# Attention scores formed one item ahead, and as one product of 128 keys instead of two of 64

## The chip, the cores and the metric

The kernel runs on one core of a Trainium2 chip. The metric is the device time of one execution in microseconds (us), as the median of several runs.

## What is computed

The first half is a linear attention with a decaying state, over batch 4, 8 heads, 768 tokens and a head dimension of 48, all in float32. The second half sends each of the 3072 tokens (384 features) to one of 8 experts.

```python
for t in range(S):                       # attention, for every batch b and head h
    cur = einsum('bhd,bhe->bhde', u * k[t], v[t])
    y[t] = einsum('bhd,bhde->bhe', r[t], state + cur)
    state = w[..., None] * state + einsum('bhd,bhe->bhde', k[t], v[t])
x = y transposed to (B, S, H * D)
logits = x @ w_gate                      # router: the best expert, or the one of the token before
out = p[e] * (relu(x @ w1[e]) @ w2[e])   # e is the token's expert, p its softmax share
```

## The kernel before

Two heads share the 128 partitions (64 each, 48 used), so an *item* is a batch and a pair of heads, and there are 16 items. An item's 768 tokens are six chunks of 128. `run` goes over the items in a loop whose order is written out by hand; each engine executes its instructions in that order, and the engines wait for each other by semaphores. After the loop come the experts, which are TensorE work almost without a break.

The steps of one item n, with the line numbers of the profile:

- `load` (L199, L203, L204, SP's queue): rk holds r and k with tokens along the free axis, kv holds k and v with tokens on the partitions, vT is v turned. It runs three items ahead.
- `scale` (GpSimd): rw = r times the decay to its place in the chunk (L234), pd = r times k (L221), ke = k times the decay to the chunk's end (L217). Items 0 to 2 get rw from VectorE. It is issued one item ahead.
- `keys` (VectorE, L241): kw = k divided by the decay.
- `added` (TensorE, L253) and `states` (VectorE, L259): what each chunk adds to the state, and the scan that makes the five states S.
- `scores` (TensorE, L288): products of kw and rw for each chunk and head, three chunks at a time (g = 0 and 1) into one of two pairs of PSUM banks; then `am` on VectorE (L290) multiplies them by the tile `kept`, which has zeros where a key doesn't come before the query.
- `own` (TensorE, L269): the token's own term, u times pd, into the PSUM tile y; VectorE multiplies it by vT in place (L273).
- `inside` (TensorE, L297): adds v times am to y. `before` (TensorE, L310): adds the states' part. Then ScalarE copies y to xT (L314). The tile y has one buffer, so own(n+1) waits for the copy of item n.
- `turn` (TensorE, L323; ScalarE, L325): xT back to tokens on the partitions, two items later, through a bank pair. After four items ScalarE's queue writes x to memory (L328), and `logits` (L336) and `token_logits` (L342) form the router's logits, also through the bank pairs.

`banks` hands out the two bank pairs in turn, so every user waits until the reader of what stood there has finished.

In iteration n the order on TensorE is: turn(n-2), added(n), inside(n-1), before(n-1), scores(n), own(n). The masked scores of item n are thus made in iteration n and used in iteration n+1. Each chunk's score product is split into two of 64 keys. The first half of the keys meets all 128 queries, the second half only the last 64, since no key comes after its query. The two halves are written to different halves of the PSUM partitions, swapped in odd chunks; so `kept` has an entry for even and one for odd chunks, and v, k and the decay table for ke come with swapped halves there (`_tokens`, `endT`).

Between these steps stand the steps of the router for the first two batches: `keys` and `runs` in iteration 10 (L679, L684), `turn_runs` at the end of 10 (L689), `last` and `one_hot` in 11, `counts` and `ranks` in 12, `slots` and `places` in 13 and 14 (L765 to L783), `summed` and `head` in 15 (L790, L800); after `head` the first tokens are gathered for the experts (L1037).

Of the kernel before, what the change touches and what calls it, by code (L numbers as in the profile page):

```python
# [11 lines left out]
F32 = mybir.dt.float32  # L12
# [8 lines left out]
P = 128  # L21
B, H, S, DH = 4, 8, 768, 48
HP = H // 2
DP = 64
U = DP + DH
D = H * DH
E, F = 8, 1024
DK, FK = D // P, F // P
NCH = S // P
NC = B * NCH  # L30
# [20 lines left out]
C2 = NCH // 2  # L51
# [4 lines left out]
def spread(ap, axis, n):  # L56

    a = ap.unsqueeze(axis)
    return a.to_broadcast([n if i == axis else s for i, s in enumerate(a.shape)])


class Attention:
# [10 lines left out]

    def __init__(self, tc, st, rk_d, kv_d, vT_d, x_d, w_t, wp_d, kept, ident, lt, mp):
        self.tc, self.nc = tc, tc.nc
        nc = tc.nc
        self.rk_d, self.kv_d, self.vT_d, self.x_d = rk_d, kv_d, vT_d, x_d
        self.w_t, self.kept, self.ident, self.lt = w_t, kept, ident, lt  # L80

        self.late = st.enter_context(tc.tile_pool(name="late", bufs=1))
        self.wp = self.late.tile([P, H, 32], F32, name="wp")
# [3 lines left out]
        def pool(name, bufs, **kw):  # L87
            return self.inner.enter_context(tc.tile_pool(name=name, bufs=bufs, **kw))

        once = pool("once", 1)  # L90
        self.two = pool("two", 2)
        self.three = pool("three", 3)
        ps = pool("ps", 1, space=PSUM)

        self.pairs = [ps.tile([P, 2, 512], F32, name=f"pair{i}") for i in range(2)]
# [7 lines left out]
        n = B * HP - 1  # L103
# [25 lines left out]
        n = 2  # L129
# [7 lines left out]
        nc.scalar.copy(self.first, tab[:, 0, 0])  # L137
        self.reciprocals(0)

        self.end = once.tile([P, HP, P + DP], F32, name="end")  # L140
        self.endT = once.tile([P, 2, HP, 2 * DH], F32, name="endT")
        self.align(26)
        self.warm(8)
        self.ends(slice(0, 1))
# [19 lines left out]
            self.nc.tensor.transpose(t[:, i % 2, :P], self.ident, self.ident)  # L164

    def ends(self, z):
        self.nc.scalar.copy(self.end[:, z, :P], self.tab[:, z, 0, P - 1::-1])
        self.nc.scalar.copy(self.end[:, z, P:], self.tab[:, z, 0, P - 1:DP - 1:-1])  # L168

    def turn_ends(self, z):  # L170
        ep, n = self.banks("ep"), z.stop - z.start
        for k in range(n):
            for o in range(2):
                self.nc.tensor.transpose(ep[:, o, k * P:(k + 1) * P], self.end[:, z.start + k, o * DP:o * DP + P], self.ident)
        self.nc.scalar.copy(self.endT[:, :, z].rearrange("p o i (h d) -> p o (i h) d", h=2),
                            ep[:, :, :n * P].rearrange("p o (i d) -> p o i d", d=DP)[..., :DH])

    def tables(self):

# [28 lines left out]
    def scale(self, n):  # L208

        nc, t = self.nc, self.items[n]  # L210
        t["ke"] = self.two.tile([P, NCH, 2 * DH], F32, name="ke")
        t["pd"] = self.two.tile([P, NCH, P], F32, name="pd")
        t["rw"] = self.three.tile([P, NCH, P], F32, name="rw")
        hp = t["hp"]

        def ke(p):
            nc.gpsimd.tensor_mul(t["ke"][:, p::2], t["k"][:, p::2], spread(self.endT[:, p, hp], 1, C2))  # L217

        def pd(i):
            z = slice(i * C2, (i + 1) * C2)  # L220
            nc.gpsimd.tensor_mul(t["pd"][:, z], t["rT"][:, z], t["kT"][:, z])  # L221

        def rw(i):
            self.decayed(nc.gpsimd, n, slice(i * C2, (i + 1) * C2))


        for what in (ke, rw, pd) if n > 2 else (pd, ke):
            for i in range(2):
                what(i)

# [44 lines left out]
    def scores(self, n, g):  # L275

        nc, t = self.nc, self.items[n]
        if g == 0:
            t["am"] = self.two.tile([P, 2, 2, 3, P], F32, name="am")
        sc = self.banks("sc")[:, :, :3 * P].rearrange("p h (c t) -> p h c t", t=P)  # L280
        for i in range(3):
            c = 3 * g + i
            for o in range(2):
                for h in range(2):
                    q, f = slice(h * DP, h * DP + DH), c % 2 ^ o

                    x = o * DP if n else 0
                    nc.tensor.matmul(sc[f * DP:(f + 1) * DP, h, i, x:], lhsT=t["kw"][q, c, o * DP:(o + 1) * DP],  # L288
                                     rhs=t["rw"][q, c, x:], start=True, stop=True)
        return lambda: nc.vector.tensor_mul(t["am"][:, g], sc, spread(self.kept[:, g:g + 3], 1, 2))  # L290

    def inside(self, n):
        nc, t = self.nc, self.items[n]
# [51 lines left out]
    def run(self, router, fetch, heads):  # L345


        def pair(name):
            t = self.banks(name)
            return [t[:, 0], t[:, 1]]  # L350

        M = B * HP

        mp, mp_end = router.mp, 2 * P + 2 + (NCH - 1) * DH

        g = GROUPS[0][1] * HP
        for n in range(M + 1):
# [19 lines left out]
            if n < 3:  # L377
# [8 lines left out]
                keep = self.scores(n, 1)  # L386
# [10 lines left out]
                continue  # L397
            if n < M:
                self.turn(n - 2, pair("tp"))
                if n == 3:  # L400
                    self.added(3)
                    self.reciprocals(3)
                self.keys(n)
                if n > 3:
                    self.added(n)
            if n == g + 2:
                router.keys(0, mp)
            if n == g + 3:
                router.last(0, mp[:, mp_end:])
            if n == g + 4:  # L410
                router.counts(0, [mp, mp[:, E * NC // 2:]])
            if n < M:
                self.states(n)
            if n > HP and n % HP == 1:
# [2 lines left out]
                self.chooser()  # L417
            if n == g + 1:
                router.experts_of(0, (0,))
            if n == g + 2:  # L420
                router.runs(0)
            if n == g + 3:
                router.one_hot(0, (0,))
            if n == g + 4:
                router.ranks(0, (0,))
            if n == g + 5:
# [10 lines left out]
            if n == M:  # L437
                self.turn(M - 2, pair("tp"))
            self.inside(n - 1)
            if n == g + 7:  # L440

                router.summed(0, 0)
                router.copied(0)
            self.before(n - 1)
            if n == 6:
                router.cast()
            if n == M:
                break
            if n == g + 7:
                router.head(pair("tb")[0])  # L450
                heads()
            self.scores(n, 0)()
            keep = self.scores(n, 1)
            if n == g + 1:
                router.experts_of(0, (1,))
            if n == g + 3:
                router.one_hot(0, (1,))
            if n == g + 5:
                router.places(0, 0)
            if n == g + 6:  # L460
                router.places(0, 1)
            if n % HP == 0:

                keep()
                self.own(n)
                self.logits(n // HP - 1, pair("lp")[0])
                if n == g + 4:
                    router.ranks(0, (1,))
            else:
                self.own(n)  # L470
                keep()
            if n == g + 2:
                router.turn_runs(0, mp[:, mp_end:])
        self.inner.close()


def general_attention(tc, rk_d, kv_d, wu, wg_d, x_d, ident, lt):

    nc = tc.nc
    with tc.tile_pool(name="g1", bufs=1) as g1, tc.tile_pool(name="g2", bufs=2) as g2, \  # L480
# [3 lines left out]
        nc.vector.memset(ones, 0.0)  # L484
        for i in range(2):
            nc.vector.memset(ones[i * DP:(i + 1) * DP, i:i + 1], 1.0)
        turned = g1.tile([P, P], F32, name="g_turned")
        nc.vector.tensor_copy(turned[:, :DP], ident[:, DP:])
        nc.vector.tensor_copy(turned[:, DP:], ident[:, :DP])
        with tc.For_i(0, HP, 1) as hp:  # L490
            wu_t = g1.tile([P, 2], F32, name="g_wu")
            nc.sync.dma_start(out=wu_t, in_=wu[bass.ds(hp, 1)].rearrange("o p x -> (o p) x"))
            with tc.For_i(0, B, 1) as b:
# [11 lines left out]
                for e in range(DH):  # L505
                    vp = gps.tile([P, 2, 512], F32, name="g_vp")
                    for c in range(NCH):
                        for i in range(2):
                            nc.tensor.matmul(
                                vp[i * DP:(i + 1) * DP, c // 3, (c % 3) * P:(c % 3 + 1) * P],  # L510
                                lhsT=v_t[:, c, i, e:e + 1].to_broadcast([P, DP]),
                                rhs=turned if c % 2 else ident,
                                start=True, stop=True)
                    kv = g2.tile([P, S], F32, name="g_kv")
                    nc.vector.tensor_mul(kv.rearrange("p (g t) -> p g t", g=2),
# [5 lines left out]
                    z = g2.tile([P, S], F32, name="g_z")  # L521
                    nc.vector.scalar_tensor_tensor(z, kv, wu_t[:, 1:2], sv[:, :S], Alu.mult, Alu.add)
                    nc.vector.tensor_mul(z, z, r_t)
                    for c in range(NCH):
                        o = (c % 3) * 2 * DH + 2 * e
                        nc.tensor.matmul(yp[:, c // 3, o:o + 2], lhsT=z[:, c * P:(c + 1) * P], rhs=ones,
                                         start=True, stop=True)
# [28 lines left out]
class Router:  # L556
# [246 lines left out]
    def heads(self, table, out):  # L803
        self.nc.vector.tensor_reduce(out, table[:, :EARLY, :2], axis=AX.X, op=Alu.add)
# [757 lines left out]
def kernel(  # L1562
# [12 lines left out]
    nc = tc.nc  # L1575
# [10 lines left out]
    nc.gpsimd.affine_select(out=mask, in_=mask, compare_op=Alu.is_ge, fill=0.0, base=-1,  # L1586
                            channel_multiplier=-1, pattern=[[1, P]])

    kept = keep.tile([P, 4, P], F32, name="kept")
    lo, hi = slice(0, DP), slice(DP, P)  # L1590
    nc.gpsimd.tensor_copy(kept[:, 0], mask)
    nc.gpsimd.memset(kept[lo, 1, lo], 0.0)
    nc.gpsimd.tensor_copy(kept[lo, 1, hi], mask[lo, lo])
    nc.gpsimd.tensor_copy(kept[hi, 1, lo], mask[hi, hi])
    nc.gpsimd.memset(kept[hi, 1, hi], 1.0)
    nc.scalar.copy(kept[:, 2:], kept[:, :2])
    lt = keep.tile([P, NC, E + 1], F32, name="lt")

    gid = keep.tile([P, E * ST], I32, name="gid")
# [4 lines left out]
    with ExitStack() as st, tc.manual_schedule():  # L1604
# [1 line left out]
        mpp = st.enter_context(tc.tile_pool(name="mpp", bufs=1, space=PSUM))  # L1606
        router = Router(tc, ro, mpp, lt, mask, ident, gid, sid, gate, over[:, 0:1])
        ex = Experts(tc, st, x_d, w1, w2, out, ident, router)
        att = Attention(tc, st, rk_d, kv_d, vT_d, x_d, w_t, wp_d, kept, ident, lt, router.mp)
        att.run(router, lambda: ex.fetch(0, nc.sync), lambda: ex.gather(0))  # L1610
        ex.open(st)
        router.open(1, st.enter_context(tc.tile_pool(name="ro1", bufs=1)))
# [49 lines left out]

def _tokens(a, np):

    x = a.reshape(B, HP, 2, NCH, 2, DP, DH)
    x = np.stack([x[:, :, :, c, ::-1 if c % 2 else 1] for c in range(NCH)], 2)
    return x.transpose(0, 1, 4, 5, 2, 3, 6).reshape(B, HP, P, NCH * 2 * DH)


# [35 lines left out]
```

## Time and profile before

| | |
|---|---|
| median of 3 runs | 388.06 us (387.67 to 389.85) |
| the profiled execution | 388.15 us, of which span 386.4 us |
| first attention product to the last logits (L288 at 7.45, L336 at 115.73) | 108 us |
| busy over the span | PE 371.5, VectorE 247.1, ScalarE 107.6, GpSimd 151.1 us |
| score products L288: records, busy | x768, 22.4 us |
| am on VectorE L290 | x32, 952 ns each |
| DMA | 74.97 MB, mean 194 GB/s, about 410 GB/s in the first 58 us |

PE busy counts the union of its records' modelled times; a record of the attention lasts about 270 ns while several run at once on different parts of the array, so counts and start times say more there than the busy share. A product in float32 leaves two records, each with a weight load, and a transpose one. Busy time is given for the whole span; the two halves of the kernel have different limits.

### The profile page before, as it was taken

Reading aid. Unit: us, or ns where it says so; the run is one execution under the profiler, and the core shown is the slowest. Engines: PE = TensorE matmul, PEld = TensorE weight load, DVE = VectorE, ACT = ScalarE, POOL = GpSimd, SP = SyncE. Lnnn points to the kernel's source line nnn. Section 1 sums busy time; section 2 is a strip of 40 time slices with the busy share of each in tenths; the row PEclk is TensorE's granted clock in tenths of the full one; section 3 lists DMA queues with packets and bytes.
Section 4 is the critical chain, followed back from the end, with each engine's and each line's share of the span. In section 5 each row is a group of like instructions: output and inputs, shape, how many; then the busy total and the mean of one; then the engine's idle time right before and its main releaser. Section 6 shows DMA issues by size and latency. Waiting matters only on the chain. (4 is left out here: it accounts for less than half of the span.)

```text
span 386.4 us, 9723 instructions
## 1 busy us (share of the span) xinstructions
PE 371.5 (96%) x3858; PEld 328.5 (85%) x3858; DVE 247.1 (64%) x718; ACT 107.6 (28%) x293; POOL 151.1 (39%) x212
## 2 busy tenths in 40 slices
PE   7999999799999999999999999999999999999992
PEld 6776877677777999998999999999999999999971
DVE  7887576588954564587657757758757758556400
ACT  4132232222213111322323233234224234222220
POOL 8769998696322022611333222312403213012022
PEclk9999999999999999999999999999999999999998
DMA  7999998979213982740552145245156146064011
GB/s 257 414 409 410 409 405 274 355 256 394 99 32 101 378 338 64 249 185 23 184 179 108 42 170 213 66 171 204 56 185 224 38 165 227 21 199 181 2 37 37
DMA packets 17477, 74.97 MB, mean 194 GB/s; under 512 B 2729, under 2 KB 6586, under 8 KB 14864
## 3 DMA queue, kind: packets, MB, share of 16 engines
q1 hardware_dynamic: 10048, 56.89, 39.1%
q0 software_dynamic: 3424, 9.52, 7.4%
q10 hardware_dynamic: 3952, 7.87, 5.6%
q8 instruction: 32, 0.52, 0.6%
q14 instruction: 21, 0.17, 0.1%
HBM read 64.83 MB, written 9.51 MB: 192 GB/s over the span
## 5 line engine op out<-in xcount | busy, mean ns | idle before, releaser
L1263 POOL DMA_INDIRECT out_dram<-yo,sid x27 | 26.6, 986 | 102.3 <-ACT yo L1258 78.8
L1114 PE MATMUL h<-exT,w1t 128*128 128x168 f32 (+4 forms) x240 | 54.9, 327 | 0.0
L1118 DVE TENSOR_TENSOR hT<-h,hs 128x168 f32<-128x168 f32 (+3 forms) x60 | 21.1, 351 | 46.5 <-PE h L1114 30.4
L1037 POOL DMA_INDIRECT xg<-x_d,gid x29 | 31.1, 1073 | 38.2 <-DVE sm L872 17.4
L1114 PEld LDWEIGHTS h<-exT,w1t 128*128 128x128 f32 x240 | 41.7, 190 | 0.3 <-issue 0.3
L290 DVE TENSOR_TENSOR am<-pair,kept 128x768 f32<-128x768 f32 x32 | 30.1, 952 | 16.8 <-PE pair L288 16.4
L1064 PE MATMUL h<-exT,w1t 128*128 128x192 f32 (+1 forms) x192 | 38.2, 337 | 0.0
L1183 PE MATMUL y<-factors,sums 128*128 128x192 f32 x168 | 36.8, 326 | 0.0
L1114 PE MATMUL h<-xs,ws 128*128 128x168 f32 (+4 forms) x144 | 35.2, 326 | 0.0
L1064 PEld LDWEIGHTS h<-exT,w1t 128*128 128x128 f32 x192 | 32.3, 190 | 1.4 <-issue 0.2
L221 POOL TENSOR_TENSOR pd<-rk 128x384 f32<-128x384 f32 x32 | 31.9, 1017 | 3.0 <-DMA rk<-in_rk_dram 2.2
L297 PE MATMUL y<-am,kv 128*64 128x128 f32 x384 | 28.9, 278 | 3.4 <-issue 2.2
L1114 PEld LDWEIGHTS h<-xs,ws 128*128 128x128 f32 x144 | 25.5, 190 | 4.3 <-ACT hs L1121 1.2
L1183 PEld LDWEIGHTS y<-factors,sums 128*128 128x128 f32 x168 | 28.9, 190 | 0.0
L297 PEld LDWEIGHTS y<-am,kv 128*64 128x64 f32 x384 | 24.8, 136 | 4.7 <-issue 2.4
L234 POOL TENSOR_TENSOR rw<-rk,tab 128x384 f32<-128x384 f32 x26 | 23.6, 931 | 7.3 <-PE y L310 7.3
L217 POOL TENSOR_TENSOR ke<-kv,endT 128x288 f32<-128x288 f32 x32 | 24.9, 799 | 3.9 <-DMA kv<-in_kv_dram 3.0
L314 ACT COPY xT<-y 128x768 f32<-128x768 f32 (+1 forms) x16 | 12.5, 779 | 42.3 <-PE y L310 42.3
L288 PE MATMUL pair<-rw,kw 48*64 48x128 f32 (+1 forms) x768 | 22.4, 249 | 1.3 <-ACT end L168 0.6
L1183 PE MATMUL y<-w2t,hT 128*128 128x192 f32 x96 | 23.0, 328 | 0.0
L1051 DVE COPY exT<-tp 128x384 f32<-128x384 f32 (+6 forms) x29 | 14.0, 489 | 12.8 <-PE tp L1050 12.6
L288 PEld LDWEIGHTS pair<-rw,kw 48*64 48x64 f32 x768 | 19.4, 133 | 2.7 <-issue 0.9
(279 smaller groups left out, 733.0 us busy)
## 6 DMA issues: line engine op xcount, KB each, us to landing
w1t<-in_w_dram SPq DMA_DIRECT2D x9, 1536.0 KB, 6.7
w2t<-in_w_dram SPq DMA_DIRECT2D x9, 1536.0 KB, 7.3
rk<-in_rk_dram SPq DMA_DIRECT2D x15, 768.0 KB, 9.4
kv<-in_kv_dram SPq DMA_DIRECT2D x16, 584.0 KB, 9.1
vT<-in_vT_dram SPq DMA_DIRECT2D x16, 384.0 KB, 7.4
x_d<-x ACTq DMA_DIRECT2D x4, 1152.0 KB, 10.7
w1t<-in_w_dram ACTq DMA_DIRECT2D x1, 1536.0 KB, 10.2
w2t<-in_w_dram ACTq DMA_DIRECT2D x1, 1536.0 KB, 13.5
```

The costliest lines, as they stand in the source:

```text
L217: nc.gpsimd.tensor_mul(t["ke"][:, p::2], t["k"][:, p::2], spread(self.endT[:, p, hp], 1, C2))
L221: nc.gpsimd.tensor_mul(t["pd"][:, z], t["rT"][:, z], t["kT"][:, z])
L234: engine.tensor_mul(t["rw"][:, z], t["rT"][:, z], spread(pw, 1, z.stop - z.start))
L288: nc.tensor.matmul(sc[f * DP:(f + 1) * DP, h, i, x:], lhsT=t["kw"][q, c, o * DP:(o + 1) * DP], rhs=t["rw"][q, c, x:], start=True, stop=True)
L290: return lambda: nc.vector.tensor_mul(t["am"][:, g], sc, spread(self.kept[:, g:g + 3], 1, 2))
L297: nc.tensor.matmul(t["y"][p * DP:(p + 1) * DP, h, c2 * P:(c2 + 1) * P], lhsT=t["v"][:, (2 * c + h) * DH:(2 * c + h) * DH + DP], rhs=t["am" ...
L1037: self.nc.gpsimd.indirect_dma_start(out=xg[:n], out_offset=None, in_=self.x_d[:rows], in_offset=bass.IndirectOffsetOnAxis(ap=u["gid"][:n, ...
L1064: nc.tensor.matmul(h[:, :n], lhsT=u["w1"][:, m, kk, :], rhs=u["xT"][:, kk, :], start=(kk == 0), stop=(kk == DK - 1))
L1114: nc.tensor.matmul(out, lhsT=a, rhs=b, start=start and k == 0, stop=stop and k == len(terms) - 1, skip_group_check=True)
L1118: nc.vector.tensor_tensor(out, a, b, op=Alu.add)
L1183: return lambda: nc.tensor.matmul(bank[:, x * half:(x + 1) * half], lhsT=a, rhs=b, start=(j == 0 and x == 0), stop=(j == FK // 2 - 1), ski ...
L1263: self.nc.gpsimd.indirect_dma_start(out=out.rearrange("n (h d) -> (n h) d", h=2) if half else out, out_offset=bass.IndirectOffsetOnAxis(ap ...
```

## The change

- Scores are one product of 128 keys by 128 queries for each chunk and head: 12 products for an item instead of 24. The halves are no longer swapped: `kept`, the second half of `end` and `endT`, and the swap in `_tokens` are gone, and am multiplies by the plain `mask`.
- From iteration 5 on, scores(n+1) are formed in iteration n instead of scores(n); iteration 4 forms those of items 4 and 5, and iteration 15 none. kw is made two items ahead (`keys(n + 2)`, behind own(n)), and rw has four buffers instead of three.
- In iterations from 5 on VectorE's order behind the scores is: am of the first half, y times vT, kw, am of the second half. `scale` for items from 5 on is in the order rw, ke, pd.
- The router's `keys` and `runs` move to the end of iteration 10, `turn_runs` into iteration 11 between turn and added; `one_hot` is in one piece, `counts` comes ahead of added, the second part of `experts_of`, `places` and `head` come behind own, and `summed` behind before.

```diff
-        self.three = pool("three", 3)
+        self.four = pool("four", 4)
...
-        for what in (ke, rw, pd) if n > 2 else (pd, ke):
+        for what in (pd, ke) if n < 3 else (ke, rw, pd) if n < 5 else (rw, ke, pd):
...
         for i in range(3):
             c = 3 * g + i
-            for o in range(2):
-                for h in range(2):
-                    q, f = slice(h * DP, h * DP + DH), c % 2 ^ o
-
-                    x = o * DP if n else 0
-                    nc.tensor.matmul(sc[f * DP:(f + 1) * DP, h, i, x:], lhsT=t["kw"][q, c, o * DP:(o + 1) * DP],
-                                     rhs=t["rw"][q, c, x:], start=True, stop=True)
-        return lambda: nc.vector.tensor_mul(t["am"][:, g], sc, spread(self.kept[:, g:g + 3], 1, 2))
+            for h in range(2):
+                q = slice(h * DP, h * DP + DH)
+                nc.tensor.matmul(sc[:, h, i], lhsT=t["kw"][q, c], rhs=t["rw"][q, c], start=True, stop=True)
+        return lambda: nc.vector.tensor_mul(t["am"][:, g], sc, spread(spread(self.mask, 1, 3), 1, 2))
...
                 self.turn(n - 2, pair("tp"))
+                if n == g + 3:
+                    router.turn_runs(0, mp[:, mp_end:])
+                if n == g + 4:
+                    router.counts(0, [mp, mp[:, E * NC // 2:]])
...
-                self.keys(n)
+                if n < 5:
+                    self.keys(n)
...
-            self.scores(n, 0)()
-            keep = self.scores(n, 1)
+            ahead = n if n < 5 else n + 1
+            if ahead < M:
+                self.scores(ahead, 0)()
+                keep = self.scores(ahead, 1)
+            if n % HP == 0:
+
+                keep()
+                self.own(n)
+                self.logits(n // HP - 1, pair("lp")[0])
+                if n == 4:
+                    self.keys(5)
+                    self.scores(5, 0)()
+                    self.scores(5, 1)()
+                    self.keys(6)
+                else:
+                    self.keys(n + 2)
+                if n == g + 4:
+                    router.ranks(0, (1,))
+            else:
+                self.own(n)
+                if 4 < n < M - 2:
+                    self.keys(n + 2)
+                if ahead < M:
+                    keep()
...
+            if n == g + 2:
+                router.keys(0, mp)
+                router.runs(0)
...
-            if n % HP == 0:
-
-                keep()
-                self.own(n)
-                self.logits(n // HP - 1, pair("lp")[0])
-                if n == g + 4:
-                    router.ranks(0, (1,))
-            else:
-                self.own(n)
-                keep()
-            if n == g + 2:
-                router.turn_runs(0, mp[:, mp_end:])
+            if n == g + 7:
+                router.head(pair("tb")[0])
+                heads()
```

Here g is 8 and M is 16. In the changed kernel the lines shift: scores L284, am L285, own L268, inside L292, before L305, added L252, turn L318, turn_runs L692.

## The prediction

> **What bounds the kernel now.** I read the page first (span, share of each engine), then the timeline through whole iterations of the attention loop, then the start times of single TensorE records inside one. Each product of float32 leaves two records on PE (L288's 384 products are x768 on the page), a transpose one.
>
> ```profile
> span 386.4 us, 9723 instructions
> PE 371.5 (96%) x3858; PEld 328.5 (85%) x3858; DVE 247.1 (64%) x718; ACT 107.6 (28%) x293; POOL 151.1 (39%) x212
> q8 instruction: 32, 0.52, 0.6%
> ```
>
> TensorE is busy all through; the experts (from 117.7 us to the end) are not touched, so only the loop's end moves the time. The next lines are iteration 7 to 8, PE's stages with what DVE and ACT do between them.
>
> ```profile
> 53.68 1.19 PE L288 MATMUL pair<-rw,kw 48*64 48x128 f32 x48
> 53.92 0.80 ACT L314 COPY xT<-y 128x768 f32<-128x768 f32 x1 [2.91 <-PE y L310]
> 54.87 0.88 PE L269 MATMUL y<-pd,w_t 48*64 48x384 f32 x8
> 55.67 0.79 PE L323 MATMUL pair<-ident,xT 112*128 112x112 f32 x6
> 55.86 0.97 DVE L273 TENSOR_TENSOR y<-y,vT 128x768 f32<-128x768 f32 x1 [0.42 <-PE y L269]
> 56.40 0.65 PE L253 MATMUL mp<-kv,ke 128*48 128x48 f32 x20
> 56.73 0.95 DVE L290 TENSOR_TENSOR am<-pair,kept 128x768 f32<-128x768 f32 x1
> 56.88 1.94 PE L297 MATMUL y<-am,kv 128*64 128x128 f32 x24
> 57.60 0.94 DVE L241 TENSOR_TENSOR kw<-rk,inv 128x768 f32<-128x768 f32 x1
> 58.75 1.30 PE L310 MATMUL y<-rw,S 48*48 48x128 f32 x20
> ```
>
> Two waits are seen. inside (L297) starts when y is masked by vT (55.86+0.97), but its second half needs the second am, which ends at 57.68: L297 takes 1.87 to L310's start, against 1.51 where nothing waits (39.34 to 40.85). And own (L269) does not follow the scores: it follows the xT copy, 0.15 after it ends (53.92+0.80, then 54.87). From L310's start to own's this is 1.89 in three clean iterations (67.02 to 68.91, 95.39 to 97.28, 101.68 to 103.57). The scores therefore lie partly under a copy.
>
> ```profile
> 74.03 1.47 PE L297 MATMUL y<-am,kv 128*64 128x128 f32 x20 [2.16 <-issue]
> 114.90 0.90 PE L310 MATMUL y<-rw,S 48*48 48x128 f32 x20
> 115.73 2.07 PE L336 MATMUL y<-xT,wp 128*32 128x384 f32 x16
> 118.54 0.84 PE L342 MATMUL y<-sel,lT 128*128 128x18 f32 x6
> ```
>
> The first line is a third kind of loss: no semaphore, PE simply had no instruction. Such gaps stand at 33.5 (0.52), 52.9 (0.25), 59.1 (0.25) and 71.9 (2.16): 3.2 us. Counted in program order (weight loads, records, semaphore instructions) they lie at PE instructions 1217, 1985, 2241 and 2753, multiples of 256 apart, and each ends 2.3 to 2.5 us after a 16 KB packet on q8 began, in the stretch where the DMA engines are nearly full. The Trainium skill, "Runtime: NRT & Kernel Launch", Instruction fetch mechanics, says that a crossing of a 256-instruction block is mostly hidden; four here were not, and by its rule the 3.2 us would not exist to be regained.
>
> **The change part by part.** (1) *The products.* Now 24 products leave 48 records on four quarters of the array (48 rows by 64 columns), 12 on each, six moving 128 columns at 0.109 and six moving 64 at 0.055: 0.98. After: 12 products, 24 records on two row halves with 128 columns, 12 on each. A record costs the longer of 128 moving columns (L297: (1.58-0.27)/12 = 0.109 on each column half) and of loading 128 weight columns (L342 moves only 18 and still takes (0.84-0.27)/5 = 0.114): 0.11, so 1.32. No row of the trace has row halves with all columns; that they overlap I take from the four quarters, whose row halves do. Bounds: 1.32 if they overlap, 2.64 if not; I take 1.32. am masks the same 768 elements at 0.95.
>
> (2) *Seams.* L310 to L336 changes the geometry (48*48 to 128*32): its last record starts at 114.90+0.63, the next group 0.20 later, where a record needs 0.11: 0.09 lost. L310 to L288 has the same geometry today and the two overlap (47.40 to 47.48). After, the scores differ from L310 before and L269 behind: two new seams an item, 0.09 each (bounds 0, as at L253 to L297, and 0.27, a whole record). The Trainium skill, "TensorEngine Tiling (Array Packing)", Key Properties, says that changing the tiling mode drains the TensorE, which speaks against this change; as a full drain it would be the upper bound.
> From L310's start: 0.63+0.20 to the first score, 11x0.11 to the last, 0.20 to own: 2.24 instead of 1.89. So +0.35 an item. In items 1 to 3 it is +0.3, +0.27 and +0.35; about 0.2 comes back at the start, where three transposes fewer stand before the first states: +0.7 by own(4), whose own +0.35 and the 0.52 gap before it make own(4) 35.5 (34.93 now).
>
> (3) *am one item early.* inside no longer waits for am: 1.51 instead of 1.87. DVE's order becomes am0(n+1), y(n), kw(n+2), am1(n+1); y then gates inside at 0.88+0.10+0.97+0.05 = 2.00 from own, while PE reaches it at 0.80+0.73+0.48 = 2.01: free. am1 ends 3.8 after own starts and the next scores need its bank at 4.35: free by 0.5. A plain iteration is 0.80+0.73+0.48+1.51+2.24 = 5.76, POOL's own 1.56+1.96+1.96 = 5.5 stays under it, and rw's fourth buffer keeps it an item ahead.
>
> (4) *The shift.* In iteration 4 item 5's scores are added. They wait for kw(5), which DVE reaches after y(4): own(4) ends 36.4, y 37.45, kw 38.35. PE is done with logits at 37.8 and stands 0.6; 1.4 for the scores; turn then waits for am0(5) (+0.6), as its bank is the one that they filled. own(5) comes at 46.1 to 46.2, against 42.74: +3.4.
>
> (5) *Router steps.* keys and runs go behind own(10) and turn_runs ahead of added(11). DVE runs the scan after y, kw and am1: 0.98+0.97+0.91+0.94+0.39 = 4.2 after own(10) starts, while PE asks at 1.8. PE stands 2.4, with added, inside and all later products behind it. Afterwards 0.13+0.55 (added)+0.35 (last)+1.51+2.24: step 10 to 11 is 9.0. Today 78.13 comes 4.7 after the scan, so nothing waits. counts ahead of added is the same work.
>
> (6) *The end.* Iteration 15 forms no scores. own(14) to own(15): 0.80+0.72+0.48, 0.45 of waiting for y behind ohq and val on DVE, 1.51, 1.89 (the copy again): 5.85 instead of 7.48. own(15) to logits 2.00+1.51+0.83 = 4.34 instead of 4.68. The gathers now start 2.75 after own(15); they took about 3.8 from issue to landing of the second, PE wants it at 6.7: just hidden, else some tenths.
>
> (7) *Hidden.* The kept mask (POOL 1.3, ACT 0.40 before 6.3 us), half of end and endT: DVE's table chain sets the start, so nothing. ke and am keep their sizes. SP's queue keeps its order; kw reads rk two iterations earlier, yet rk lands at most 11.4 after an issue that is three items ahead (27.57 for item 7, read near 47). If that margin went, each lost us would be a us.
>
> **Sum.** own to own now, from item 5: 5.94, 6.19, 6.19, 7.85, 8.42, 6.10, 6.13, 7.72, 6.29, 7.48, and 4.68 to the logits at 115.73: 72.99. After: 5.76 three times; 8.06 (5.76 with 1.43 logits, 0.77 token logits and a seam); 5.76 (the 2.16 gap gone); 9.0; 6.3 (5.76 and 0.55 counts); 8.06; 5.76; 5.85; 4.34: 70.4. So -2.6, and +3.4 at own(5): +0.8. A plain item is 208 PE instructions instead of 256, so a block lasts 256/208x5.76 = 7.1 us instead of about 6: one us more for each fetch, which covers the three gaps under 0.6. The gap of 2.16, with x's write just ahead, would keep about 1.1 if it met a block end again; I give that one chance in four: 0.3. The profiled run is 388.15 (span 386.4 and 1.75 around it; median of the three 388.06): 388.15+1.1 = 389.2.
>
> **Rivals.** *Faster: the scores stay under the copy.* If they start while L310 drains, as 48 rows by 64 columns do today, own is again at 1.89: -0.35 in some 12 iterations, 385.0. For it: quarters overlap now. Against: every change of geometry in this loop shows 0.09.
> *Slower: the seams drain.* At 0.27 instead of 0.09, twice in 15 items: +5.4, 394.6. For it: the geometry is new here. Against: three seams of 0.09. It decides above 0.12 a seam, where the sum passes +0.5%.
> *Slower: fetch gaps return* at the new block ends with about what they cost now, +3: 392. *Row halves do not overlap:* +1.3 in 16 items, 410. That the scores are not formed ahead is excluded by the order of the instructions.
>
> **Numbers.** 0.5% is 1.9 us, about what a measurement of this kernel can tell from no change. Forecast 0.42 (its own range 387.4 to 391.0), under the copy 0.20, draining seams 0.20, fetch gaps 0.12, no overlap 0.06. Faster 0.20; within 0.40; slower 0.40 (0.20+0.10+0.06 and the forecast's upper edge). The range goes from the faster rival to the draining seams, 384.8 to 394.6.
>
> **What would show it.** L285's waits for PE should shrink and L292 take 1.51; from L305's start to L268's 2.24 (1.89 or 2.6 decide the rivals); scores of 24 records over 1.2 (2.6: no overlap); own(5) near 46.2; a PE gap of 2.4 ahead of L692; gaps with no semaphore only at blocks of 256. I am wrong if L292 still waits on DVE, or if the loop's logits lie over 3 us from 116.5.

## The result, and the profile after

The changed kernel takes 394.11 us (median of 6 runs, 393.78 to 398.17) against 388.3 of the kernel before, which ran beside it: the ratio is 1.0158, 95% interval 1.0129 to 1.0187. It is slower by about 6 us, or 1.6%. The profiled execution took 394.13 us with a span of 392.4. The page of the changed kernel, whose rows answer to those of before (busy time of the engines, the granted clock in 40 slices, instruction fetches):

```profile
span 392.4 us, 8917 instructions
...
PE 377.0 (96%) x3470; PEld 332.8 (85%) x3470; DVE 249.7 (64%) x718; ACT 106.4 (27%) x290; POOL 149.6 (38%) x207
...
PEclk9999999989999999999999999999999999999998
...
q8 instruction: 29, 0.48, 0.5%
```

TensorE has 388 records fewer and is busy 5.5 us longer. The one 8 inside the row of the clock is new: in slice 9 (78 to 88 us) the clock was not fully granted. The timeline of a plain item (6 to 7), start, duration, engine and line, as it was shown of before:

```profile
51.97 1.61 PE L284 MATMUL pair<-rw,kw 48*128 48x128 f32 x24
52.08 0.80 ACT L309 COPY xT<-y 128x768 f32<-128x768 f32 x1 [2.14 <-PE y L305]
...
53.51 0.87 PE L268 MATMUL y<-pd,w_t 48*64 48x384 f32 x8
...
54.50 0.97 DVE L272 TENSOR_TENSOR y<-y,vT 128x768 f32<-128x768 f32 x1 [0.59 <-PE y L268]
...
55.52 1.58 PE L292 MATMUL y<-am,kv 128*64 128x128 f32 x24
56.24 0.95 DVE L285 TENSOR_TENSOR am<-pair,mask 128x768 f32<-128x768 f32 x1
57.04 0.90 PE L305 MATMUL y<-rw,S 48*48 48x128 f32 x20
```

Inside (L292) no longer waits: 1.52 to L305's start, though VectorE makes an am at 56.24, in the middle of it, for that am belongs to the next item. Own (L268) no longer follows the copy of xT, which ended at 52.88, but the scores: it starts 2.37 after L305 (51.14). From own to own a plain item takes 5.90 (47.60, 53.51, 59.40, 65.30); before it was 5.94, and 6.19 twice with a fetch gap of 0.25. Two places are much worse. The timeline at items 5 and 11:

```profile
39.65 1.61 PE L284 MATMUL pair<-rw,kw 48*128 48x128 f32 x24 [0.84 <-DVE kw L240]
41.64 0.80 PE L318 MATMUL pair<-ident,xT 112*128 112x112 f32 x6 [0.38 <-DVE am L285]
...
83.00 0.40 DVE L687 TENSOR_TENSOR_SCAN run<-mp,seg 12x128 f32<-12x128 f32 x1
83.45 0.23 PE L692 MATMUL mp<-ident,run 12*128 12x12 f32 x1 [2.40 <-DVE run L687]
...
84.89 2.47 PE L292 MATMUL y<-am,kv 128*64 128x128 f32 x24
```

The steps from own(5) to the logits are 5.91, 5.89, 5.90, 8.20, 5.89, **10.89**, 6.30, 8.19, 5.99, 5.42, 4.36: 72.9, as much as before (73.0). In step 10 to 11 TensorE waits 2.40 for the scan, and then inside takes 2.40 from its start to L305's instead of 1.52, with nothing that it waits for. Windows of that stretch (busy time and count of each engine, granted clock, DMA share, GB/s) show why:

```profile
81.05:83.45 2.40, 0.01 (x1) 0.00 (x0) 2.35 (x4) 0.70 (x2) 2.40 (x4) 1.00 0.73 273
83.45:85.00 1.55, 1.24 (x25) 1.10 (x27) 0.00 (x1) 0.17 (x1) 0.82 (x2) 1.00 1.02 371
85.00:88.80 3.80, 3.80 (x46) 3.11 (x46) 1.79 (x7) 0.00 (x0) 1.35 (x2) 0.55 0.35 104
```

The column behind the five engines is the granted clock: 1.00, 1.00, then a mean of 0.55. In windows of 0.1 us it is 0.50 from 85.36 to 88.78 and 1.00 on both sides: 3.41 us at half speed, at most 1.7 us lost, and they begin 1.9 us after the wait had ended. Own(5) comes at 47.60 (42.74 before), the logits at 120.54 (115.73 before).

### The profile page after: what moved, and what is told of

It is laid out like the page before. It is cut to its first block, busy times and chain, and to the rows that moved or that the text cites. A ratio compares the mean times of both kernels' runs of the same rounds, so it can differ in the third digit from the quotient of the medians.

```text
span 392.4 us, 8917 instructions
## 1 busy us (share of the span) xinstructions
PE 377.0 (96%) x3470; PEld 332.8 (85%) x3470; DVE 249.7 (64%) x718; ACT 106.4 (27%) x290; POOL 149.6 (38%) x207
## 5 line engine op out<-in xcount | busy, mean ns | idle before, releaser
L285 DVE TENSOR_TENSOR am<-pair,mask 128x768 f32<-128x768 f32 x32 | 30.0, 951 | 14.1 <-PE pair L284 14.1
L284 PE MATMUL pair<-rw,kw 48*128 48x128 f32 x384 | 26.3, 282 | 1.4 <-DVE kw L240 0.8
L292 PE MATMUL y<-am,kv 128*64 128x128 f32 x384 | 26.8, 284 | 0.9 <-DVE y L272 0.9
L284 PEld LDWEIGHTS pair<-rw,kw 48*128 48x128 f32 x384 | 23.0, 188 | 4.9 <-POOL t_i L605 1.5
L292 PEld LDWEIGHTS y<-am,kv 128*64 128x64 f32 x384 | 22.9, 140 | 1.3 <-DVE y L272 1.2
L309 ACT COPY xT<-y 128x768 f32<-128x768 f32 (+1 forms) x16 | 12.5, 778 | 40.5 <-PE y L305 40.5
```

The source lines that it names most:

```text
L284: nc.tensor.matmul(sc[:, h, i], lhsT=t["kw"][q, c], rhs=t["rw"][q, c], start=True, stop=True)
L292: nc.tensor.matmul(t["y"][p * DP:(p + 1) * DP, h, c2 * P:(c2 + 1) * P], lhsT=t["v"][:, (2 * c + h) * DH:(2 * c + h) * DH + DP], rhs=t["am" ...
```

## The experiments

**The router's scan at its old place.** The wait at item 11 is taken away by giving the scan the places that it had before; the second part of `experts_of`, whose result it needs, goes ahead to where the first part stands.

```diff
             if n == g + 1:
-                router.experts_of(0, (0,))
+                router.experts_of(0)
...
-                if n == g + 3:
-                    router.turn_runs(0, mp[:, mp_end:])
...
+            if n == g + 2:
+                router.keys(0, mp)
...
+            if n == g + 2:
+                router.runs(0)
...
             if n == g + 2:
-                router.keys(0, mp)
-                router.runs(0)
+                router.turn_runs(0, mp[:, mp_end:])
```

> The changed kernel with the router's scan (keys, runs, turn_runs) back at the places that it had before the change: all of experts_of in iteration 9 behind states, keys behind added(10), runs behind states(10), turn_runs behind own(10). Theory: step 10 to 11 took 10.89 us because TensorE waits 2.4 us for the scan and then runs at a granted clock of 0.75 to 0.80 for 7.6 us, about 1.7 us more; without the wait both go: step 10 to 11 about 6.5, granted clock 1.0 there, total 394.1 - 4.1 = 390.0. Rival A, the low clock has another cause than the wait (it would come at that time anyway): 391.7 and a clock under 0.9 in that stretch. Rival B, the wait is given back at the next late step (last, one_hot, counts): over 393.

Measured: 389.64 us, ratio to before 1.0033 (1.0016 to 1.005), 4.5 less than the changed kernel. Step 10 to 11 is 6.47 (79.41 to 85.88), TensorE waits nowhere in it, and the clock is 1.00 from 75 to 91 us:

```profile
75.00:91.00 16.00, 16.00 (x280) 13.08 (x276) 13.52 (x22) 4.19 (x11) 13.87 (x17) 1.00 0.89 325
```

So the one misplaced step costs 4.4 us, wait and clock together; neither rival holds. It is not the profiled execution alone: the mean granted clock is 0.994 to 0.997 in all ten executions here, and 0.980 to 0.991 in all six of the changed kernel.

**The wait filled with work.** The scan stays late; TensorE is only kept busy.

```diff
                 if n == g + 3:
+                    for i in range(18):
+                        self.nc.tensor.transpose(self.pairs[0][:, i % 2, 3 * P:], self.ident, self.ident)
                     router.turn_runs(0, mp[:, mp_end:])
```

> The changed kernel with 18 transposes of the identity into unused columns of the bank ahead of turn_runs in iteration 11: TensorE works about 2 us in the place where it waited 2.4 us, and turn_runs comes at the same time. Theory: the low clock after that wait comes from the idle time itself; filled, the clock stays at 1.0 and the 1.7 us go: 392.4, with a rest of the wait of about 0.4. Rival, the clock falls for another reason: 394.1, with the clock at 0.75 to 0.80 behind turn_runs as now.

Measured: 393.0, ratio 1.0143 (1.0107 to 1.0178), 1.1 less than the changed kernel, by useless work. The timeline and windows of this run:

```profile
81.47 2.19 PE L397 MATMUL pair<-ident 128*128 128x128 f32 x18 [0.79 <-ACT x L320]
83.59 0.23 PE L694 MATMUL mp<-ident,run 12*128 12x12 f32 x1
...
85.00:88.80 3.80, 3.80 (x69) 3.44 (x69) 2.21 (x8) 0.80 (x1) 1.47 (x2) 1.00 0.43 123
```

The clock stays at 1.00. From turn_runs (L694) to own(11) it is now 5.32 instead of 6.83, so the low clock had cost 1.5. Step 10 to 11 falls by 1.0 only, from 10.89 to 9.88, because turn_runs comes 3.65 behind the start of turn instead of 3.14: the transposes start 0.79 late, behind the copies that read their bank, and run past the scan's end. With TensorE kept busy the clock holds: the idle time itself brings the low clock. One of the four executions, which was not the profiled one, took 395.79 at a mean clock of 0.986 (the others 0.995 to 0.997), so filling most of the wait did not keep the clock up every time.

**kw(5) earlier.** `self.keys(5)` moves from behind own(4)'s logits to behind states(4).

> The changed kernel with kw(5) formed behind states(4), where VectorE is idle for 1.46 us, in place of behind own(4). Theory: the wait of 0.84 for kw(5) goes and am0(5) comes sooner too; own(5) at about 46.7 in place of 47.60, total 393.2. Rival, the next thing is as late (the copy of the logits, whose bank the second half of the scores takes, or am0(5)): own(5) over 47.2, total 393.7 or more.

Measured: 393.36, ratio 1.0128 (1.0101 to 1.0155). Own(4) to own(5) falls from 11.09 to 10.20, as expected, and own(5) comes at 46.34. What is left of the wait is 0.30 for am at L318. But in the profiled execution, of 393.73 us, step 10 to 11 rises to 11.76 with the same wait of 2.40 for the scan:

```profile
40.37 0.80 PE L318 MATMUL pair<-ident,xT 112*128 112x112 f32 x6 [0.30 <-DVE am L285]
...
82.19 0.28 PE L693 MATMUL mp<-ident,run 12*128 12x12 f32 x1 [2.40 <-DVE run L688]
```

```profile
81.30:88.10 6.80, 5.61 (x65) 5.08 (x67) 2.39 (x9) 0.17 (x1) 3.04 (x4) 0.50 0.45 172
```

Here the clock was 0.50 from 81.3 to 88.1 us, 6.83 us, twice as long as in the changed kernel, which gives most of the 0.9 back. Two of the four executions (393.73 and 394.13, mean clock 0.987) are like that; the other two (392.98 and 392.99) have 0.990 and 0.991, the clock of the changed kernel, and keep the gain. So the same wait has not always the same price.

**The old product in the new order.** Scores ahead and all steps moved, but two products of 64 keys with `kept` and the swapped halves.

```diff
-            for h in range(2):
-                q = slice(h * DP, h * DP + DH)
-                nc.tensor.matmul(sc[:, h, i], lhsT=t["kw"][q, c], rhs=t["rw"][q, c], start=True, stop=True)
+            for o in range(2):
+                for h in range(2):
+                    q, f = slice(h * DP, h * DP + DH), c % 2 ^ o
+                    x = o * DP if n else 0
+                    nc.tensor.matmul(sc[f * DP:(f + 1) * DP, h, i, x:], lhsT=t["kw"][q, c, o * DP:(o + 1) * DP],
+                                     rhs=t["rw"][q, c, x:], start=True, stop=True)
```

> The changed kernel's order (scores one item ahead, all moved steps) with the product as it was before: two products of 64 keys on four quarters of the array, the mask kept, the swapped token halves. Theory: what a plain item lost is the product's length and its two changes of geometry; with the old product own follows the copy of xT again, 1.89 after L305's start in place of 2.37, and a plain item falls from 5.90 to about 5.5 (5.42 on TensorE, 5.5 on GpSimd, whose three steps of an item are then the bound); over 13 items about -5: 389 to 390, up to 392 if gaps of instruction fetch come back at 256 instructions an item. Rival, the order of VectorE's and GpSimd's work sets the item: plain item stays at 5.8 or more and the total over 393.

Measured: 388.27 (387.49 to 392.17), ratio 1.0015 (0.9988 to 1.0041): 5.8 less than the changed kernel, from the product alone. The timeline of a plain item, in the profiled execution of 389.29:

```profile
54.58 0.79 PE L310 MATMUL y<-rw,S 48*48 48x128 f32 x18
...
55.52 0.80 ACT L314 COPY xT<-y 128x768 f32<-128x768 f32 x1 [2.14 <-PE y L310]
...
56.38 0.88 PE L269 MATMUL y<-pd,w_t 48*64 48x384 f32 x8
```

L310 to own is 1.80, own again follows the copy (56.32), and an item takes 5.34 (45.71, 51.05, 56.38, 61.71), 0.56 less than with 128 keys. The order alone is thus worth something, and loses it at item 11: 2.37 of waiting and a clock of 0.50 from 79.3 to 86.2 us make that step 11.68.

**The new product in the old order.** The kernel before with nothing but the product of 128 keys (and `mask`, plain `_tokens`, one half of `endT`).

> The kernel before with nothing changed but the product: one of 128 keys on row halves in place of two of 64 on quarters, with the mask and the plain token order that go with it; scores in their own item, router steps at their old places. Theory: own comes 2.37 after L305's start in place of 1.89, in 16 items, +0.48 each, 7.7; with 208 PE instructions an item in place of 256 the fetch gaps (3.2 us before) mostly go: +4.5 to +6, 392.7 to 394.2. Rival, the longer product lies under the waits of inside for am that this order has, and costs nothing: 385 to 388.

Measured: 391.2, ratio 1.0062 (1.0037 to 1.0087). L305 to own is 2.37 here too, inside keeps its 1.87 of before, and plain steps rise to 6.26; the gaps of 2.16 and 0.52 are gone. The product costs 2.9 net, more than the rival's nothing and less than I expected; I had not summed the steps one by one.

**Both mended steps, 128 keys; and with 64 keys.** The first two edits that helped (scan back, kw(5) early) on the changed kernel, and the same with the old product.

> The changed kernel with both mended steps together: the router's scan at its old places and kw(5) behind states(4), product of 128 keys kept. Theory: the gains of the two runs before add up, -4.5 and -0.8: 388.8; what is left of the change's two halves, order and product, then cancels against the kernel before. Rival, the half clock needs only little idle time and stays somewhere: over 390.

> Scores one item ahead with the old product of 64 keys, the router's scan at its old places, and kw(5) formed behind states(4): what the runs so far point to. Theory: the three gains add up. With the old product 388.27; less 5.8 for steps 9 to 11 (17.2 us to 11.4: the wait of 2.4 and the half clock go), less 0.9 at own(5): 381.6, logits near 109.1 in place of 115.79. Rival, the loads of rk or GpSimd's steps become the bound when TensorE goes faster (the DMA share is near 1.0 until about 83 us): 384 to 386. Rival, fetch gaps come back at 256 instructions an item: one of about 2 us, 383.5.

Measured with 128 keys: 388.65, ratio 0.9998 (0.9973 to 1.0023); gains add up (5.5 in all). With 64 keys: 384.85, ratio **0.9896** (0.987 to 0.9921): faster than both kernels, yet 3 us behind the 381.6 that were expected. Its profiled execution took 389.62 and the six others 383.8 to 385.0, so it was profiled again:

> The run with all three steps once more, for a second profile: the time at 384.9; L678's duration and TensorE's wait for am(10) are expected shorter than in the first profile (3.22 and 3.07), and the granted clock at 1.0 behind it if the wait is under 2.2.

The second execution took 383.75. Timelines, first of the execution of 389.62, then of that of 383.75:

```profile
66.21 3.22 DVE L678 TENSOR_TENSOR eq<-lt,mx 128x96 f32<-128x96 f32 x1
...
72.83 1.38 PE L323 MATMUL pair<-ident,xT 112*128 112x112 f32 x6 [3.07 <-DVE am L290]
```

```profile
65.64 2.63 DVE L678 TENSOR_TENSOR eq<-lt,mx 128x96 f32<-128x96 f32 x1
...
66.60 1.56 POOL L217 TENSOR_TENSOR ke<-kv,endT 128x288 f32<-128x288 f32 x2
...
69.36 1.96 POOL L221 TENSOR_TENSOR pd<-rk 128x384 f32<-128x384 f32 x2 [1.21 <-PE y L269]
...
70.18 0.79 PE L323 MATMUL pair<-ident,xT 112*128 112x112 f32 x6 [0.99 <-DVE am L290]
```

A comparison of 96 elements, 0.59 in the changed kernel and 0.72 before, takes 2.63 and 3.22 here. It ends at 68.27, 0.11 after GpSimd's queue came to its first pause (66.60 + 1.56 = 68.16). The am behind it is late, and TensorE waits 0.99 or 3.07. After 0.99 the clock stays 1.00; with 3.07 it was 0.50 from 72.0 to 78.8 us, and the step took 11.39 instead of 6.70. That is the same program with and without the halved clock, its logits 5.3 us apart. In the faster execution, too, the steps with router work on VectorE keep 5.9 to 6.7 us while plain ones fall to 5.34: from own(9) to own(11) it is 12.6 where the expectation had 11.4. Another 1.0 is a slip in its sum: it took the 5.8 us seen in an execution of 389.29 off the median of 388.27. The rest is not explained. The time lies in the range of the rival that loads or GpSimd become the bound; plain items, however, take 5.33 to 5.39, no longer than in the run before, so no such bound shows there.

**The router's chain later.** A try at that: runs behind am1(11), turn_runs ahead of own(11), and what follows one iteration later.

> As the run with all three steps (scores ahead, product of 64 keys, early kw(5)), but the router's chain is put later instead of back: the second half of experts_of behind am1(10), keys ahead of own(10), runs behind am1(11), turn_runs ahead of own(11), last and one_hot in iteration 12, counts ahead of own(12), ranks behind it. Theory: what kept that run at 384.85 in place of 381.6 is VectorE: the seven instructions of experts_of took 5.9 us there instead of 2.3 (one of them, L678, 3.22), because GpSimd has no gap in that stretch, so am(10) came late and TensorE waited 3.07 for its bank. With only the first four of them ahead of am(10) that wait falls to 1 or less and no clock is lost: 382.0, range 381 to 383. Rival, the loads or GpSimd's three steps are the bound: 384.5 or more.

Measured: 390.16, ratio 1.0067 (1.0039 to 1.0095), a miss, on the rival's side of 384.5. The timeline:

```profile
79.17 0.40 DVE L695 TENSOR_TENSOR_SCAN run<-mp,seg 12x128 f32<-12x128 f32 x1
...
79.67 0.66 PE L253 MATMUL mp<-kv,ke 128*48 128x48 f32 x20 [2.51 <-POOL rw L234]
```

am(10) did come sooner (a wait of 0.36), but now added waits 2.51. The row names rw on GpSimd; yet added reads no rw, its ke was ready at 75.5, and it starts 0.10 after the scan ends. The keys that the scan reads lie in the bank mp that added writes. I read it so; no run with another bank was made. The wait had only changed its place, with a low clock behind it again.

## Why the prediction was right and wrong

The total, 394.1, lies inside the range but 4.9 above the forecast of 389.2. That it lies inside is luck: the upper edge, 394.6, was the price of draining seams (5.4), and the seams gave only some 1.6 more than forecast (0.13 in 12 items); most of the miss has other causes. One of the prediction's own signs of being wrong did come: the loop's logits are at 120.54, 4.0 from 116.5, where it allowed 3. Point by point:

- **Products (1)**: right. The row halves overlap; score records start 0.112 apart (52.18 to 53.30 for ten steps). The rival without overlap is out.
- **Seams (2)**: mis-sized. The first score record starts 0.20 after L305's last, as said, but then takes 0.37 instead of 0.27, and the second starts 0.21 after it; own follows the last by 0.21. That is three losses of 0.10 where the step put two of 0.09, so 2.37 instead of 2.24. By the sum for both seams, 0.30, this is beyond the 0.12 each from which the rival of draining seams was to decide. Own's tie to the copy, 1.89 with quarters, came back with the old product (1.80): the rival "under the copy" fell with the geometry.
- **am early (3)**: right, L292 1.52 with no wait. A plain item is 5.90 instead of 5.76 through the seam alone.
- **The shift (4)**: mis-sized, +4.86 instead of +3.4 at own(5). The waits were named rightly (0.84 for kw(5) and 0.38 for am, where the step had 0.6 each). Own(4) comes at 36.51 instead of 35.5: own(0) was 0.57 later, not earlier (about 0.2 in the three runs that share this kernel's start), and items 1 to 3 lost 0.2 to 0.5 each. The run with kw(5) early gives 0.9 of it back.
- **Router steps (5)**: the wait of 2.4 was right to the figure, and the step still failed: 10.89 instead of 9.0. I had seen the gap of 2.16 before the change pass without harm and took it that idle time costs its length. The filled and the removed wait show the missing term: a half clock, 1.5 us between turn_runs and own(11) (6.83 against 5.32). The remaining 0.4 lies between turn_runs and added, 0.53 (83.45 to 83.98, 0.30 of it idle) for the 0.13 of the sum.
- **The end (6)**: 5.42 and 4.36 for 5.85 and 4.34. Behind the logits 0.4 more is lost (the xT copy at L309 starts 1.36 after L305 instead of 0.95), and 0.8 in the experts, where ACT's L1070 comes 2 us after its product had ended. The two executions of the same program above show that 0.8 in one and not in the other; its cause is open.
- **Fetch gaps**: right that they mostly go; none above 0.3 is left in the loop, and the 0.3 set aside for one was not needed. That the longer blocks did it is not shown: in the four profiled executions with 64 keys in the new order, 256 instructions an item as before, the gap of 2.16 did not come back either; of the gaps with no semaphore, one of 0.24 to 0.61 near 34 us stayed.

The miss of 4.9 is 1.0 at own(4), 0.45 at own(5), 2.5 in the steps behind it (1.9 of them at item 11), 0.4 and 0.8 behind the logits, less 0.3. In the mended order the product of 128 keys costs 3.8 us (388.65 against 384.85); order and early am gain 3.4 (384.85 against 388.3); the two misplaced waits took 5.5.

## What to carry to other kernels

Of a step that is moved to an in-order queue, price the wait, then ask what the wait does to the engine's clock: 2.4 us of an idle TensorE cost 4.4 here. Fewer, larger products are not cheaper when the smaller ones overlapped the products ahead of them and lay under a copy. When a change mixes a good part with bad ones, run the parts alone: here the order was worth 3.4 us and the product it came with took all of it.

## What the runs showed of the hardware

- **The clock falls to half for one or two spells of 3.41 us.** In windows of 0.1 us every low stretch in the loop has a clock of 0.50 and a length of 3.41 (changed kernel) or 6.83 (kw(5) early, old product in the new order, the execution of 389.62); the late chain had one of each. They begin between 0.9 us before and 1.9 us after the end of a wait. The waits were 2.37 to 3.07 us, and once 1.59 (late chain, added at 97.03); the 2.16 of the kernel before had none, nor had 0.99. So the length of a wait alone does not decide. The places tell more: in each trace the clock changes only whole multiples of 3.413 us after it first came to 1.00, in the kernel before from 4.92 to 383.80 (111.0 of them), in the changed kernel from 6.86 to 85.36 (23.0). In the window of this grid ahead of each low spell of the loop TensorE had stood for 1.50 to 2.47 us; the 2.16 lies across a border, 1.31 on one side and 0.85 on the other. The two windows of the kernel before, then the one ahead of the low spell and the spell in the changed kernel:

```profile
69.77:73.19 3.42, 2.11 (x33) 1.55 (x32) 3.42 (x6) 0.70 (x2) 3.24 (x4) 1.00 1.03 403
73.19:76.60 3.41, 2.56 (x66) 2.39 (x69) 0.26 (x1) 0.22 (x1) 0.40 (x2) 1.00 1.06 376
```

```profile
81.95:85.36 3.41, 1.60 (x31) 1.46 (x32) 1.81 (x4) 0.17 (x1) 2.68 (x4) 1.00 0.85 307
85.36:88.78 3.42, 3.42 (x42) 2.73 (x38) 1.43 (x7) 0.00 (x0) 0.99 (x2) 0.50 0.29 78
```

While the clock was at 1.00 in the loop, no window with 1.31 or less of idle time was followed by a low one. How sharp the limit is stays open: behind the last products of two runs, windows with 1.57 and 1.75 (by the modelled ends of the records) were not followed by one at once. The grid lies differently in each execution (the first 1.00 comes at 4.25 to 7.58 us), which fits that one wait costs a spell, two or none. Of the 19 executions of the kernel before that ran beside the product of 128 keys in the old order, the three longest (390.70 to 391.98) have a mean clock of 0.986 to 0.990, the others 0.994 to 0.997; whether there the 2.16 fell into one window is not shown, as none of the three was profiled. What makes a spell double is open: in the late chain the second half followed on 3.41 us (97.74 to 101.15) in which TensorE never stood. The Trainium skill, "TensorE: Matmul & The Clock Gate", Part 1, describes a full and a half clock, set by the activity in a free-running window of 3413 ns: the half, the length and the shifting place agree. Its advice in the same part, under HAM oscillation, no idle gap above about 3.4 us, does not: 1.50 us were enough where they lay within one window.
- **VectorE behind GpSimd.** A comparison that reads two SBUF operands (eq<-lt,mx) took 0.26 us where GpSimd stood (before, at 120.02) and 0.47 to 3.22 us in the loop, the long ones where GpSimd had no pause: those of 1.68, 2.63 and 3.22 us (old product in the new order and the two executions above) each end 0.11 to 0.12 after GpSimd's last instruction ahead of a pause. The Trainium skill, "SBUF — State Buffer", Who interferes with whom, says that such an instruction and a GpSimd one that reads SBUF exclude each other. These ends agree, though the 2.63 outlasted several GpSimd instructions; L241, with two such operands too, took 0.94 throughout.
